# Spreading a decay by transfers from DRAM instead of products with ones, and moving a pair's loads behind a weights piece

## The chip, the cores and the metric

The kernel runs on one core of one Trainium2 chip. The metric is device time in microseconds. Before the change three runs gave 350.66, 350.76 and 352.0 us; their median is 350.76 us.

## The reference, cut to what matters

Two blocks, one behind the other: a Mamba-2 scan (SSD) in chunks, and a feed-forward block with a quick GELU.

```python
batch, n_heads, seq, head_dim, d_state = (4, 8, 768, 32, 16); chunk = 32
for c in range(nc):
    la = log(clip(a))[:, :, sl];  cum = cumsum(la)          # decay a: (batch, head, seq)
    L  = exp(cum[i] - cum[j]) * causal                      # decay between two steps of a chunk
    y  = (C @ B^T * L) @ x + (C @ state) * exp(cum)         # inside the chunk + from the state
    state = exp(sum(la)) * state + sum_j B_j x_j exp(cum[-1] - cum[j])
x = y.transpose(0, 2, 1, 3).reshape(batch * seq, 256)       # 3072 rows
h = x @ w_in;  out = (h * sigmoid(1.702 * h)) @ w_out       # 256 -> 2048 -> 256
```

All data are float32 in meaning. The two weights come as 64-bit floats, and the kernel makes float32 of them itself.

## The kernel before

**Tiles.** The 3072 rows are worked in six groups of 512 (`TG`), and the sequence of a batch in chunks of 128 rows that hold two halves of 64. A *pair* is two such chunks, 256 rows, so a group has two pairs (`PG`) and there are twelve pairs, p0 to p11. A batch is three pairs: p0, p1 and p2 belong to batch 0. "Third pair" is p2 (in the code `PG`), "fourth pair" is p3 (`PG + 1`). Each group's scan gives `yT`, which is multiplied with `w_in` (`hidden` for group 0, a Strassen-like scheme `first` for the others), passed through Silu and multiplied with `w_out` (`project_all` for group 0, `product` for the others).

**The order is written out by hand.** Instructions stand on each engine in the order in which the program calls them, and `in_order` at the end fixes it. Lists such as `in_hidden[0]` and `in_project[0]` say which extra work stands behind the f-th step of group 0's `hidden` loop (16 steps, f = 0 to 15), or ahead of the f-th step of `project_all`. All loads of this part go through one queue, SyncE's (SP).

**Weights.** `fetch(i)` loads piece i (two transfers), `fields(i)`, `rounded(i)` and `join(i)` turn it into float32 on VectorE, with two steps on ScalarE between them (`clamp(i)`). `narrow(i)` is rounded(i), fields(i+1), join(i). Pieces 0 to 5 are `w_in`, pieces 6 to 9 are `w_out`; each of pieces 6 to 9 is 1 MB and holds four f-steps of `project_all`. Pieces, and the spread `a` of most pairs, share four buffers (tag `bits`).

**What the pair's scan needs.** `L`, the decay between two steps, for all heads in all 128 partitions (512 numbers for each half). For most pairs it is made so: `store_a` clips all of `a` (in `az`), sets the first of every 64 to zero and writes it to DRAM (`scratch`); `spread(p)` reads a pair's part back with two transfers, each spreading the same rows over 64 partitions (`a<-scratch`, 256 KB each); `decay(p)` runs one scan over it (L402) and `ends(p)` (L461) makes `Be`, B times the decay to the end of the half. For p2 it is made without DRAM: `pick_a` (L366, ScalarE) puts each head's rows beside zeros, `fan` (L412, TensorE) multiplies them with ones, which spreads them over the partitions in PSUM, and `decay_heads` (L450) scans them from there, a fourth at a time.

**Rows of a.** `since[b]` is the decay since the start of each half, by batch, in a layout of 8 heads x 16 states over the partitions. For batches 1 to 3 `spread_rows(b)` loads a's rows so spread (`af<-in_a_dram`, 384 KB), `clip_rows` clips them (L480) and moves the first of each half aside on POOL (L485, L486), `decay_rows` scans them (L493). For batch 0 the first four chunks come from `since_first`, and the last two chunks (those of p2) from `fan_since`: two products with a matrix of ones by head (L501, L530), then a copy and a scan on VectorE (`since_fanned`, L541, L543).

**What comes behind.** `turn(p)` transposes a pair's b and c on TensorE (L597, four products into one bank of PSUM, `tp`), copies them to SBUF on ScalarE (L590) and makes `CsT` from `tp` and `since` on VectorE (L667). `score` (L682) and `gain` (L713) are the products of a pair of pairs; `finish` (L821, L833) gives y; `keep_both` and `add_up` carry the states; `weigh` (L693) multiplies L with the scores.

**The queue around the change.** SP's order is: az (4 transfers, L272), piece 6, p2's b, b, c, c, x, x, scratch (2), piece 7, piece 8, p3's b, b, c, c, x, x, piece 9, p3's a (2), batch 1's af, p4's a. An issue can wait for a semaphore of an engine (a buffer that is still read) and for the landing of the eighth transfer before it. `load(p)` issues b, c and x, in two transfers each; these move rows of 64 bytes (b, c) or 128 bytes (x).

Of the kernel before, what the change touches and what calls it, by code (L numbers as in the profile page):

```python
# [16 lines left out]
P = 128  # L17
# [18 lines left out]
def kernel(  # L36
# [68 lines left out]

    az = ffn.tile([P, 4 * TG // 2], FP32, tag="mg", name="az", bufs=3)[:, :NC * P].rearrange(
        "p (c s) -> p c s", c=NC)
# [137 lines left out]
    def spread(p, held=False):  # L245

        if p - 2 in ra:
            ra[p] = ra[p - 2]
        else:
            ra[p] = words(f"a{p}").bitcast(FP32)[:, :2 * NH * H].rearrange(  # L250
                "p (k e) -> p k e", k=2)
        if held:
            nc.vector.memset(ra[p][:, 0, :1], 0.0)
        b, c = divmod(2 * p, NC)
        for i, side in enumerate(SIDES):
            nc.sync.dma_start(
                out=ra[p][side],
                in_=scratch[c:c + 2, i, b * NH:(b + 1) * NH].rearrange("c h i -> c (h i)").unsqueeze(
                    0).to_broadcast([H, 2, NH * H]))
# [3 lines left out]
    def spread_rows(b):  # L263
        raf[b] = raw.tile([P, NC, P], FP32, tag="af", name=f"af{b}", bufs=1)
        nc.sync.dma_start(out=raf[b].rearrange("p c s -> p (c s)"),
                          in_=a[b].unsqueeze(1).to_broadcast([NH, N, S]))

    def rows_a(t, queues):

        e = t.shape[1] * P  # L270
        for r in range(R):
            queues[r % len(queues)].dma_start(  # L272
                out=t[32 * r:32 * r + 32].rearrange("p c s -> p (c s)"),
                in_=a.rearrange("b h s -> (b h) s")[:, :e])

# [72 lines left out]

    starts, fans, flat = {}, {}, {}

    def clip(t, name):

        nc.vector.tensor_scalar(out=t, in0=t, scalar1=1e-6, scalar2=1.0,
                                op0=ALU.max, op1=ALU.min)
        starts[name] = const.tile([P, t.shape[1], 2], FP32, name=f"starts{name}")
        first = t.rearrange(by_chunk, s=2)[:, :, :, 0]
        nc.vector.tensor_copy(starts[name], first)
        nc.vector.memset(first, 0.0)

    def pick_a(p):  # L360

        b, c = divmod(2 * p, NC)
        X = ffn.tile([P, 2, DM], FP32, tag="ob", name=f"X{p}")
        X = fans[p] = X.rearrange("p k (q i) -> p k q i", q=Q)
        for q in range(Q):
            nc.scalar.activation(X[:, :, q], az[:, c:c + 2], AF.Copy, scale=pick[:, b, q:q + 1])  # L366


# [7 lines left out]
        fill=0.0, base=N - 1, channel_multiplier=-1)  # L376
    pick = picker("pick", NB, 1, NH)
    whose = const.tile([32 * PG, 1 + PG, NH, N], FP32, name="whose")
    nc.gpsimd.memset(whose, 1.0)
    for i, n, head in ((0, 1, PG), (1, 2, PG), (0, 0, 1)):  # L380
        t = whose[32 * i:32 * i + 32, n:n + 1]
        nc.gpsimd.affine_select(out=t, in_=t, pattern=[[-1, 1], [-head, NH], [0, N]],
                                compare_op=ALU.is_equal, fill=0.0, base=-max(n - 1, 0),
                                channel_multiplier=1)
# [22 lines left out]

    def fan(p, r, ab):

        rows = slice(32 * r, 32 * r + 32)  # L410
        for i, side in enumerate(SIDES):
            nc.tensor.matmul(out=ab[side].rearrange("p (k q i) -> p k q i", k=2, q=Q),  # L412
                             lhsT=ones[rows, side], rhs=fans[p][rows][:, :, :, side],
                             start=True, stop=True, tile_position=(32 * r, H * i),
                             skip_group_check=True)

    def fan_all(p):

        ab = area(f"ab{p}")[:, :, :2 * Q * H]
        for r in range(R):  # L420
            fan(p, r, ab[:, r])
        fan_since()
        for r in range(R):
            decay_heads(p, r, ab[:, r])
        for k in range(2):
            ends(p, k)

    def pads(n, t):
# [6 lines left out]
    def keep_busy(n, m):  # L435
# [8 lines left out]
    def decay_heads(p, r, ab):  # L444

        if r == 0:
            L = ssd.tile([P, R, 2 * Q * H], FP32, tag="L", name=f"L{p}", bufs=3)
            flat[p] = L
            Ls[p] = L.rearrange("p r (k q i) -> p k r q i", k=2, q=Q)
        nc.vector.tensor_tensor_scan(  # L450
            out=flat[p][:, r], data0=ab,
            data1=idents.rearrange("p h i -> p (h i)")[:, :2 * Q * H],
            initial=0.0, op0=ALU.mult, op1=ALU.add)

# [23 lines left out]
    def clip_rows(b):  # L478
        t = raf[b]
        nc.vector.tensor_scalar(out=t, in0=t, scalar1=1e-6, scalar2=1.0,  # L480
                                op0=ALU.max, op1=ALU.min)
        first = ssd.tile([P, NC, P], FP32, tag="first", name=f"first{b}", bufs=1)
        nc.gpsimd.memset(first, 0.0)
# [5 lines left out]
    def decay_rows(b):  # L489

        t, first = raf.pop(b), firsts.pop(b)
        since[b] = ssd.tile([P, NC, P], FP32, tag="since", name=f"since{b}")
        nc.vector.tensor_tensor_scan(  # L493
            out=since[b].rearrange("p c s -> p (c s)"), data0=t.rearrange("p c s -> p (c s)"),
            data1=first.rearrange("p c s -> p (c s)"),
            initial=0.0, op0=ALU.mult, op1=ALU.add)

    def fan_rows(t, c0, c1, o):

        o = o[:, :(c1 - c0) * P]  # L500
        nc.tensor.matmul(out=o, lhsT=whose[:32, 0].rearrange("p h n -> p (h n)"),  # L501
                         rhs=t[:32, c0:c1].rearrange("p c s -> p (c s)"), start=True,
                         stop=True, tile_position=(0, 0), skip_group_check=True)
        return o

    def since_first():
# [3 lines left out]
        for p in range(PG):  # L510
            at = slice(32 * p, 32 * p + 32)
            nc.tensor.matmul(out=rows[p],
                             lhsT=whose[at, 1 + p].rearrange("p h n -> p (h n)"),
                             rhs=cum[at].rearrange("p k s -> p (k s)"), start=True, stop=True,
                             tile_position=(32 * p, 0), skip_group_check=True)
# [4 lines left out]
    def drops():  # L520
# [3 lines left out]
                1).to_broadcast([P, Q * D, 2 * CG - 1]))  # L524

    def fan_since():
        o = bank("rows4")
        t = fanned["rows"] = fan_rows(az, CG, NC, o)
        f = fanned["starts"] = o[:, 2 * P:2 * P + 2 * (NC - CG)]
        nc.tensor.matmul(out=f, lhsT=whose[:32, 0].rearrange("p h n -> p (h n)"),  # L530
                         rhs=starts[1][:32, CG:].rearrange("p c s -> p (c s)"), start=True, stop=True,
                         tile_position=(0, 0), skip_group_check=True)

    fanned = {}

    def since_fanned():

        t, f = fanned["rows"], fanned["starts"]
        first = ssd.tile([P, NC, P], FP32, tag="first", name="first0", bufs=1)[:, CG:]
        nc.gpsimd.memset(first, 0.0)  # L540
        nc.vector.tensor_copy(first.rearrange(by_chunk, s=2)[:, :, :, 0],  # L541
                              f.rearrange("p (c s) -> p c s", s=2))
        nc.vector.tensor_tensor_scan(  # L543
            out=since[0][:, CG:].rearrange("p c s -> p (c s)"), data0=t,
            data1=first.rearrange("p c s -> p (c s)"), initial=0.0, op0=ALU.mult, op1=ALU.add)

# [37 lines left out]
    def area(name):  # L584
        return psa.tile([P, R, 4 * P], FP32, tag="cb", name=name)
# [603 lines left out]
    for i in range(2, 6):  # L1189
        fetch(i)  # L1190
    rows_a(az, (nc.sync,))
    weigh(1)
# [18 lines left out]
    join(1)  # L1211
    load(PG)


# [5 lines left out]
    def store_a():  # L1220
        clip(az, 1)
        for i, side in enumerate(SIDES):
            nc.sync.dma_start(out=scratch[:, i].rearrange("c r i -> r c i"), in_=az[:32, :, side])

    at(in_hidden[0], 5, store_a, lambda: fetch(7), lambda: fetch(8),
       lambda: load(PG + 1))
    at(in_hidden[0], 6, lambda: pick_a(PG))
    at(in_hidden[0], 9, lambda: fan_all(PG))
    at(in_hidden[0], 9, since_fanned)
    for i, k, c in ((2, 1, 1), (3, 2, 2), (4, 4, 4), (5, 6, 8), (6, 9, 12), (7, 12, 15)):  # L1230
        at(in_hidden[0], k, lambda i=i: narrow(i))
# [213 lines left out]
```

## Time and profile before

| what | time |
|---|---|
| median of three runs | 350.76 us |
| the profiled execution, its own time | 349.68 us |
| its span, first to last instruction | 347.8 us |
| VectorE busy | 253.5 us |
| ScalarE busy | 153.1 us |
| POOL busy | 12.9 us |
| granted TensorE clock | 1.0 |

The span is what the profiler shows from the first to the last instruction; the execution's own time has 1.88 us more around it. Times in the views count from the start of the span. A line of a timeline is: start, length, engine, source line, operation, what it writes and reads, shape, how many; in brackets how long the engine had been idle before it and what ended that. PE is TensorE's matmul, PEld its weight load, DVE VectorE, ACT ScalarE, SPq the queue of SyncE. The length of an issue on SPq is the time that the issuing took, not the transfer.

### The profile page before, as it was taken

The page shows a single profiled execution, that of the slowest core. Times are in us where ns is not written, and L with a number is a line of the kernel's source. Part 1 is how long each engine was busy: PE and PEld are TensorE (multiplying, and loading weights), DVE is VectorE, ACT ScalarE, POOL GpSimd, SP SyncE. Part 2 cuts the span into 40 slices and gives each one's busy share as a digit, 9 for nine tenths or more (in the row PEclk, how much of TensorE's full clock was granted, in tenths as well). Part 3 has the DMA queues.
Part 4 walks back from the last instruction along what each step waited for, and adds up shares of the span by engine and source line. Part 5 has one row for each costly group of instructions (what it writes and reads, how often), then busy time and mean ns, then how long its engine had stood idle before and what let it go on. Part 6 is the DMA issues. An engine that isn't in the chain of part 4 may idle for free.

```text
span 347.8 us, 8141 instructions
## 1 busy us (share of the span) xinstructions
PE 342.0 (98%) x3392; PEld 271.9 (78%) x3392; DVE 253.5 (73%) x479; ACT 153.1 (44%) x349; POOL 12.9 (4%) x41
## 2 busy tenths in 40 slices
PE   8899999999999999999999999999999999999996
PEld 6644444557788888888888888888888888899996
DVE  5899999998679998839995649787555654455463
ACT  5698573107354324744332543442444321554320
POOL 8300000000000100000000000000000000000000
PEclk9999999999999999999999999999999999999999
DMA  6699997435526100435613036300000300000301
GB/s 162 142 336 193 283 212 155 81 77 93 105 58 128 33 2 15 63 104 102 101 28 50 2 81 117 64 2 1 2 2 2 61 2 0 0 2 0 62 0 61
DMA packets 89980, 25.92 MB, mean 75 GB/s; under 512 B 73432, under 2 KB 87128, under 8 KB 89944
## 3 DMA queue, kind: packets, MB, share of 16 engines
q1 hardware_dynamic: 89112, 24.88, 33.3%
q10 hardware_dynamic: 832, 0.52, 0.5%
q8 instruction: 26, 0.43, 0.5%
q14 instruction: 10, 0.08, 0.1%
HBM read 22.15 MB, written 3.24 MB: 73 GB/s over the span
## 4 chain that ended last, share of the span: by engine, by line
PE 97%; ACT 1%; DVE 1%; issue 0%; DVEq 0%
PE acc L1050 28%; PE X L945 20%; PE Y L955 14%; PE h L889 10%; PE o L987 8%; PE acc L1057 7%; PE y L833 2%; PE y L821 2%; PE cb L682 2%; PE A L713 1%; PE busy L440 1%; PE ab L554 1%; PE ab L548 0%; DVE steps L735 0%; ACT steps L730 0%; ACT drop L522 0%
## 5 line engine op out<-in xcount | busy, mean ns | idle before, releaser
L950 ACT ACTIVATE ac<-X 128x256 f32<-128x256 f32 x76 | 29.1, 383 | 78.6 <-PE X L945 78.2
L1050 PE MATMUL acc<-mg,mw 128*128 128x256 f32 x192 | 54.5, 379 | 0.0
L922 ACT ACTIVATE gT<-gT 128x512 f32<-128x512 f32 (+1 forms) x76 | 39.3, 520 | 34.1 <-DVE gT L1077 33.4
L1077 DVE TENSOR_TENSOR gT<-Y,ac 128x512 f32<-128x512 f32 x38 | 26.2, 689 | 36.1 <-PE Y L955 30.5
L945 PE MATMUL X<-my,mi 128*128 128x256 f32 x152 | 45.2, 380 | 0.0
L1077 DVE TENSOR_TENSOR gT<-Y,b 128x256 f32<-128x256 f32 x38 | 15.8, 419 | 35.2 <-PE Y L955 35.2
L1050 PEld LDWEIGHTS acc<-mg,mw 128*128 128x128 f32 x192 | 36.5, 190 | 5.0
L1050 PE MATMUL acc<-gT,w_out 128*128 128x256 f32 x128 | 35.5, 379 | 0.0
L889 PE MATMUL h<-yT,w_in 128*128 128x512 f32 (+2 forms) x98 | 35.5, 518 | 0.0
L945 PEld LDWEIGHTS X<-my,mi 128*128 128x128 f32 x152 | 28.0, 190 | 4.1 <-ACT ac L950 0.4
L889 PEld LDWEIGHTS h<-yT,w_in 128*128 128x128 f32 x98 | 17.0, 190 | 16.5 <-issue 14.3
L987 PE MATMUL o<-gT,w_out 128*128 128x512 f32 x64 | 28.6, 597 | 0.0
L913 DVE TENSOR_TENSOR mg<-gT 128x512 f32<-128x512 f32 x40 | 27.2, 681 | 0.0
L1050 PEld LDWEIGHTS acc<-gT,w_out 128*128 128x128 f32 x128 | 24.2, 190 | 3.4 <-ACT yT L860 0.2
L950 ACT ACTIVATE b<-X 128x256 f32<-128x256 f32 x38 | 14.6, 384 | 20.0 <-PE X L945 19.6
L945 PE MATMUL X<-yT,w_in 128*128 128x256 f32 x76 | 23.2, 389 | 0.0
L945 PE MATMUL X<-my,w_in 128*128 128x256 f32 x76 | 22.7, 382 | 0.2 <-issue 0.2
L955 PE MATMUL Y<-yT,w_in 128*128 128x256 f32 x76 | 22.7, 381 | 0.0
L955 PE MATMUL Y<-my,mi 128*128 128x256 f32 x76 | 22.6, 379 | 0.0
L955 PE MATMUL Y<-yT,mi 128*128 128x256 f32 x76 | 22.5, 379 | 0.0
L987 PEld LDWEIGHTS o<-gT,w_out 128*128 128x128 f32 x64 | 11.8, 190 | 13.2 <-issue 12.7
L402 DVE TENSOR_TENSOR_SCAN L<-a,idents 128x1024 f32<-128x1024 f32 x9 | 20.5, 2277 | 0.4 <-DMA a<-scratch 0.4
(156 smaller groups left out, 544.2 us busy)
## 6 DMA issues: line engine op xcount, KB each, us to landing
a<-scratch SPq DMA_DIRECT2D x18, 256.0 KB, 5.3
bits<-in_moe_w_out_dram SPq DMA_DIRECT2D x8, 512.0 KB, 5.4
x<-in_x_dram SPq DMA_DIRECT2D x24, 128.0 KB, 3.0
out_dram<-ob SPq DMA_DIRECT2D x40, 64.0 KB, 1.9
bits<-in_moe_w_in_dram SPq DMA_DIRECT2D x8, 256.0 KB, 4.6
bits<-in_moe_w_in_dram SPq DMA_DIRECT2D x4, 512.0 KB, 9.3
b<-in_B_dram SPq DMA_DIRECT2D x20, 64.0 KB, 3.0
af<-in_a_dram SPq DMA_DIRECT2D x3, 384.0 KB
```

The source lines that it names most:

```text
L402: nc.vector.tensor_tensor_scan(out=L, data0=ra[p].rearrange("p k e -> p (k e)"), data1=idents.rearrange("p h i -> p (h i)"), initial=0.0, ...
L682: nc.tensor.matmul(out=s["cb"][side, r, k].rearrange("p (q i) -> p q i", q=Q), lhsT=BT[rows, k, side], rhs=CT[rows, k, :, side], start=Tru ...
L889: nc.tensor.matmul(out=h[:, cols], lhsT=w_in[:, f, k], rhs=yT[g][:, k, cols], start=(k == 0 and e == 0), stop=(k == NK - 1), skip_group_ch ...
L913: nc.vector.tensor_tensor(out=t[:, 0:2], in0=B[:, :, 1], in1=B[:, 0], op=ALU.subtract)
L922: nc.scalar.activation(o, i, AF.Silu, scale=GELU_SCALE)
L945: nc.tensor.matmul(out=s["X"], lhsT=lhsT, rhs=rhs, start=i == "1", stop=i == "4", skip_group_check=True)
L950: nc.scalar.activation(copy, s["X"], AF.Copy)
L955: nc.tensor.matmul(out=o, lhsT=lhsT, rhs=rhs, start=s.pop("new", False), stop=i != "5", skip_group_check=True)
L987: nc.tensor.matmul(out=o[c], lhsT=w_out[:, c, f], rhs=gT[g, f // 2][:, f % 2], start=(f == 0), stop=(f == NF - 1), skip_group_check=True)
L1050: nc.tensor.matmul(out=acc[g][0][i][:, cols], lhsT=w, rhs=h[:, cols], start=(j == 0 and k == 0 and (i, 0) in begins), stop=(j == NF // 2 - ...
L1057: nc.tensor.matmul(out=o[k] if type(o) is list else o[:, cols], lhsT=h[:, cols], rhs=w, start=(j == 0 and (i, k) in begins), stop=(j == NF ...
L1077: nc.vector.tensor_tensor(out=o, in0=v, in1=w, op=ALU.add)
```

## The change

Three things are done, all in the first 60 us.

1. The spread of p2's `a` and of batch 0's last two chunks of rows is no longer made by products. `az` shrinks from four copies in 128 partitions to one in 32, with one load instead of four. `pick_a`, `fan`, `fan_all`, `decay_heads`, `fan_rows`, `fan_since`, `since_fanned`, `clip` and the tile `pick` go. p2's `a` is read back from `scratch` with `spread(PG)` into a buffer of the tag `yT`, and scanned by `decay(PG)` ahead of `fields(9)`. Batch 0's last rows come with `spread_rows(0)` (256 columns, 128 KB), issued right behind `load(PG)`, and `clip_rows(0)`, `decay_rows(0)` stand where the products' scans stood.
2. `load(PG + 1)`, p3's b, c and x, moves from behind piece 8 to behind piece 9 in SP's queue.
3. At the first step of `project_all` the order on VectorE becomes rounded(8), join(8), fold_ident(1), decay(PG), fields(9); before it was rounded(8), fold_ident(1), fields(9), join(8).

SP's order after is: az (1), piece 6, p2's b, b, c, c, x, x, af of batch 0 (1), scratch (2), piece 7, piece 8, p2's a (2), piece 9, p3's b, b, c, c, x, x, p3's a (2), batch 1's af, p4's a.

```diff
     def spread(p, held=False):
-        if p - 2 in ra:
+        if p == PG:
+            ra[p] = ffn.tile([P, NK, TG], FP32, tag="yT", name=f"a{p}").rearrange(
+                "p (k x) s -> p k (x s)", k=2)
+        elif p - 2 in ra and p - 2 > PG:
             ra[p] = ra[p - 2]
...
     def spread_rows(b):
-        raf[b] = raw.tile([P, NC, P], FP32, tag="af", name=f"af{b}", bufs=1)
+        c = 0 if b else CG
+        raf[b] = raw.tile([P, NC, P], FP32, tag="af", name=f"af{b}", bufs=1)[:, c:]
         nc.sync.dma_start(out=raf[b].rearrange("p c s -> p (c s)"),
-                          in_=a[b].unsqueeze(1).to_broadcast([NH, N, S]))
+                          in_=a[b, :, c * P:].unsqueeze(1).to_broadcast([NH, N, S - c * P]))
...
-    rows_a(az, (nc.sync,))
+    nc.sync.dma_start(out=az.rearrange("p c s -> p (c s)"), in_=a.rearrange("b h s -> (b h) s"))
...
     load(PG)
+    spread_rows(0)
...
     def store_a():
-        clip(az, 1)
+        nc.vector.tensor_scalar(out=az, in0=az, scalar1=1e-6, scalar2=1.0, op0=ALU.max, op1=ALU.min)
+        nc.vector.memset(az.rearrange(by_chunk, s=2)[:, :, :, 0], 0.0)
         for i, side in enumerate(SIDES):
-            nc.sync.dma_start(out=scratch[:, i].rearrange("c r i -> r c i"), in_=az[:32, :, side])
-    at(in_hidden[0], 5, store_a, lambda: fetch(7), lambda: fetch(8),
-       lambda: load(PG + 1))
-    at(in_hidden[0], 6, lambda: pick_a(PG))
-    at(in_hidden[0], 9, lambda: fan_all(PG))
-    at(in_hidden[0], 9, since_fanned)
+            nc.sync.dma_start(out=scratch[:, i].rearrange("c r i -> r c i"), in_=az[:, :, side])
+    at(in_hidden[0], 5, store_a, lambda: fetch(7), lambda: fetch(8))
+    at(in_hidden[0], 6, lambda: spread(PG))
+    at(in_hidden[0], 9, lambda: clip_rows(0), lambda: decay_rows(0))
...
-    at(in_hidden[0], 9, lambda: spread(PG + 1), lambda: spread_rows(1))
+    at(in_hidden[0], 9, lambda: load(PG + 1), lambda: spread(PG + 1), lambda: spread_rows(1))
...
-    at(in_project[0], 0, lambda: turn(PG), lambda: rounded(8), lambda: fold_ident(1),
-       lambda: fields(9), lambda: join(8))
+    at(in_project[0], 0, lambda: turn(PG), lambda: rounded(8), lambda: join(8),
+       lambda: fold_ident(1), lambda: decay(PG), lambda: fields(9))
```

More of the change, by code (lines that the diff above doesn't have):

```diff
@@ L103 @@
     dram = ctx.enter_context(tc.tile_pool(name="dram", bufs=1, space=bass.MemoryType.DRAM))
-    az = ffn.tile([P, 4 * TG // 2], FP32, tag="mg", name="az", bufs=3)[:, :NC * P].rearrange(
+    az = ffn.tile([P, 4 * TG // 2], FP32, tag="mg", name="az", bufs=3)[:32, :NC * P].rearrange(
         "p (c s) -> p c s", c=NC)
@@ L263, in spread_rows @@
     def spread_rows(b):
-        raf[b] = raw.tile([P, NC, P], FP32, tag="af", name=f"af{b}", bufs=1)
+        c = 0 if b else CG
+        raf[b] = raw.tile([P, NC, P], FP32, tag="af", name=f"af{b}", bufs=1)[:, c:]
         nc.sync.dma_start(out=raf[b].rearrange("p c s -> p (c s)"),
-                          in_=a[b].unsqueeze(1).to_broadcast([NH, N, S]))
[L268 to L274, printed above, removed]
+                          in_=a[b, :, c * P:].unsqueeze(1).to_broadcast([NH, N, S - c * P]))
     for r in range(R):
@@ L347 @@
         data1=cum.rearrange("p k s -> p (k s)"), initial=0.0, op0=ALU.mult, op1=ALU.add)
[L349 to L366, printed above, removed]
+    flat = {}
     same = ssd.tile([P, NH, D], FP32, tag="BT", name="same")
@@ L376 @@
         fill=0.0, base=N - 1, channel_multiplier=-1)
-    pick = picker("pick", NB, 1, NH)
-    whose = const.tile([32 * PG, 1 + PG, NH, N], FP32, name="whose")
+    whose = const.tile([32 * PG, PG, NH, N], FP32, name="whose")
     nc.gpsimd.memset(whose, 1.0)
[L380 to L383, printed above, removed]
+    for n in range(PG):
+        t = whose[32 * n:32 * n + 32, n:n + 1]
+        nc.gpsimd.affine_select(out=t, in_=t, pattern=[[-1, 1], [-PG, NH], [0, N]],
+                                compare_op=ALU.is_equal, fill=0.0, base=-n,
                                 channel_multiplier=1)
@@ L406, in decay @@
             ends(p, k)
[L408 to L426, printed above, removed]
     def pads(n, t):
@@ L442, in keep_busy @@
                              start=True, stop=True, skip_group_check=True)
[L444 to L453, printed above, removed]
     def ends(p, k):
@@ L481, in clip_rows @@
                                 op0=ALU.max, op1=ALU.min)
-        first = ssd.tile([P, NC, P], FP32, tag="first", name=f"first{b}", bufs=1)
+        first = ssd.tile([P, NC, P], FP32, tag="first", name=f"first{b}", bufs=1)[:, NC - t.shape[1]:]
         nc.gpsimd.memset(first, 0.0)
@@ L491, in decay_rows @@
         t, first = raf.pop(b), firsts.pop(b)
-        since[b] = ssd.tile([P, NC, P], FP32, tag="since", name=f"since{b}")
+        if b not in since:
+            since[b] = ssd.tile([P, NC, P], FP32, tag="since", name=f"since{b}")
         nc.vector.tensor_tensor_scan(
-            out=since[b].rearrange("p c s -> p (c s)"), data0=t.rearrange("p c s -> p (c s)"),
+            out=since[b][:, NC - t.shape[1]:].rearrange("p c s -> p (c s)"), data0=t.rearrange("p c s -> p (c s)"),
             data1=first.rearrange("p c s -> p (c s)"),
             initial=0.0, op0=ALU.mult, op1=ALU.add)
[L498 to L504, printed above, removed]
     def since_first():
@@ L512, in since_first @@
             nc.tensor.matmul(out=rows[p],
-                             lhsT=whose[at, 1 + p].rearrange("p h n -> p (h n)"),
+                             lhsT=whose[at, p].rearrange("p h n -> p (h n)"),
                              rhs=cum[at].rearrange("p k s -> p (k s)"), start=True, stop=True,
@@ L524, in drops @@
                 1).to_broadcast([P, Q * D, 2 * CG - 1]))
[L526 to L545, printed above, removed]
     def mask(t, new):
```

## The prediction

> **What bounds the kernel now.** I read the page first (engines and chain), then the chain of waits between 33 and 66 us, where the edits lie, then VectorE's and SyncE's timelines there, and last the transfer rates of two stretches.
>
> ```profile
> PE 342.0 (98%) x3392; PEld 271.9 (78%) x3392; DVE 253.5 (73%) x479; ACT 153.1 (44%) x349; POOL 12.9 (4%) x41
> PE 97%; ACT 1%; DVE 1%; issue 0%; DVEq 0%
> ```
>
> TensorE is busy for 98% of the span and is 97% of the chain that ended last. So a TensorE instruction that goes is worth its time, unless TensorE then waits for something that it never met before.
>
> ```profile
> 35.31 0.62 PE ab L412 x16
> 35.93 0.62 PE rows L501 x2
> 36.55 0.12 PE rows L530 x2
> 36.67 10.50 PE h L889 x24
> ...
> 51.04 0.44 PE tp L597 x4
> ...
> 64.63 0.72 PE A L713 x47
> ```
>
> Chain of waits: start, length, work. The three upper rows are the products that go. After them come two places where TensorE needs somebody else: the transposes of the fourth pair (51.04, they need its b and c loads) and gain (64.63, L713).
>
> ```profile
> 37.66 2.43 DVE L450 TENSOR_TENSOR_SCAN L<-ab,idents 128x256 f32<-128x256 f32 x4
> 40.12 0.50 DVE L461 TENSOR_TENSOR Be<-b,L 128x128 f32<-128x128 f32 x2
> 41.34 1.20 DVE L208 SCALAR_TENSOR_TENSOR m<-bits,m 128x1024 f32<-128x1024 uint32 x1
> ...
> 51.28 0.42 DVE L667 TENSOR_TENSOR CsT<-tp,since 128x256 f32<-128x256 f32 x1 [0.38 <-PE tp L597]
> ...
> 57.26 2.28 DVE L402 TENSOR_TENSOR_SCAN L<-a,idents 128x1024 f32<-128x1024 f32 x1
> 59.57 0.49 DVE L461 TENSOR_TENSOR Be<-b,L 128x128 f32<-128x128 f32 x2
> 59.98 0.55 DVE L480 TENSOR_SCALAR af<-af 128x768 f32<-128x768 f32 x1
> 61.09 1.76 DVE L493 TENSOR_TENSOR_SCAN since<-af,first 128x768 f32<-128x768 f32 x1 [0.55 <-POOL af L486]
> 62.98 0.42 DVE L667 TENSOR_TENSOR CsT<-tp,since 128x256 f32<-128x256 f32 x1
> ```
>
> VectorE here runs nearly without a gap; from 37.66 to 63.40 its three idle pieces are 0.38, 0.21 (before the last weights piece, 53.65) and 0.55. It is a second chain just behind TensorE's.
>
> ```profile
> 35.42 2.11 SPq L180 DMA_DIRECT2D bits<-in_moe_w_out_dram  x4
> 37.58 3.48 SPq L150 DMA_DIRECT2D b<-in_B_dram  x2
> 41.10 3.01 SPq L150 DMA_DIRECT2D c<-in_C_dram  x2
> ...
> 45.72 1.08 SPq L180 DMA_DIRECT2D bits<-in_moe_w_out_dram  x2
> 46.90 1.30 SPq L256 DMA_DIRECT2D a<-scratch  x2
> ```
>
> ```profile
> 48.50:50.50 2.00, 2.00 (x6) 0.81 (x5) 1.97 (x2) 1.97 (x4) 0.00 (x0) 1.00 1.04 355
> 51.00:56.50 5.50, 5.50 (x18) 2.63 (x17) 4.97 (x7) 2.34 (x3) 0.00 (x0) 1.00 1.05 190
> ```
>
> The last two columns are the DMA engines' busy share and GB/s. Both stretches are full (1.04, 1.05), yet weights (48.5 to 50.5) come at 355 GB/s and the spreads of a and af (51.0 to 56.5) at 190.
>
> **The change, step by step.** Times "after" are estimates from these rows; a shift is after minus before for the same work.
>
> *Products removed.* From 35.31 to 36.67 TensorE does nothing else, and the next h needs only a bank that ScalarE has freed. Shift of TensorE from there: -1.36. ScalarE's two picks (L366, 0.91 at 33.11) go too; ScalarE then has idle gaps at 38 to 43, so they are worth nothing more. Three of the four az loads go from SP (0.46 each) and POOL's set-up of pick; SP spends that on af0 (0.7) and a's two issues (1.3). All of it lies beside TensorE.
>
> *VectorE up to the third pair's CsT (L667 at 51.28).* The copy of starts (slot 32.71 to 32.94, 0.23) goes. The work from 37.66 to 41.34 (3.68) becomes: clip of af0, 256 columns, between the 0.17 of a 12-column copy and the 0.55 of 768 columns, taken as 0.25; the wait for POOL's copy and memset as at 61.09, 0.55; the scan, 0.61 (its slot at 40.73). 1.41 in all, so work on the weights starts at 41.34 - 0.23 - 2.27 = 38.84. Its fields step then wants piece 7 at 39.95, which lands about 40.6 (second issue 35.92, about 4.7 to landing): 0.65 lost. Pieces 6 and 7 (4.72 and 4.84 by the timeline) end at 49.05. But CsT must wait for ScalarE's copies of tp (they end 51.25), and those follow the last h on TensorE: 51.25 - 1.36 = 49.89. So VectorE idles 0.8 and its shift there is -1.36 whatever it saved before. If af0 lands up to 0.8 late, that idle time covers it.
>
> *VectorE after that.* The third pair's scan and its two Be now stand behind join(8): 2.72 (slots of 57.26 and 59.57), less the 0.21 wait for the last piece, which comes earlier. Shift at the clip of af1: -1.36 + 2.72 - 0.21 = +1.15, so 61.13, and CsT of the fourth pair ends at 63.40 + 1.15 = 64.55. In the built program gain's second matmul waits for just that CsT (it takes over the bank of tp). Gain started at 64.63; TensorE cannot be earlier than about there. **So VectorE alone takes the 1.36 back: shift about 0.0 at gain.** Bounds: -0.3 (clip 0.17, no loss at piece 7: those fall into the idle anyway, so only ScalarE's end moves it) to +1.2 (a, af1 late, below). Later meetings have more room: finish at 72.42 waits for a weigh that ended 70.95, the next gain at 83.86 for Be that ended 82.6.
>
> *The queue.* SP's order after piece 8 is now: a of the third pair (2 issues, waiting for scratch to land), last weights piece (2), then the fourth pair's b, b, c, c, x, x, then its a, af1. So 512 KB of spread and 1 MB of weights come ahead of c; before, they came behind it. What is queued behind a's wait on SP is that whole list; SP waits there some 0.3 us only, since scratch (second issue 34.9, and small transfers land 1.9 to 2.7 after their issue) lands about when piece 8's issue ends (37.2 to 37.5).
> Before: piece 8 lands at 43.6 (issue 37.0 + 6.6 in the DMA view of that issue), the second c is issued at 43.5 and lands 2.7 later (the quickest of the four c loads: 2.7/3.9/5.1), 2.6 behind the piece. The small loads hold the queue, so c follows the last big load by that 2.6. After: 43.6 + a 512 KB at 190 GB/s (2.8) + weights 1 MB at 355 GB/s (2.9) + 2.6 = 51.9. TensorE wants it at 51.3 - 1.36 = 49.95. Stall 1.95, **shift +0.6.**
> The trace has no spread in that place, so bounds: low, a at 355 GB/s (1.5): c at 50.6, shift -0.7. High, a at the 4.0 us that the spread alone at 69.5 needed (71.5, when b had landed, to 75.5) and the weights at the 5.0 of the last piece in before (two landings 2.2 and 2.8 apart): c at 55.2, shift +3.9. I take the 190 row: same kind of transfer, same fullness.
> The Trainium skill ("DMA: Bandwidth & Descriptors", Bandwidth) puts HBM's limit per core at about 358 GB/s and tells of no slower rate for a spread. The weights row agrees, the spread's row (190) doesn't; by the page c would land at 50.6 and the shift would be -0.7.
> *Late behind c:* x, a and af1 of the fourth pair. Before, af held SP's next zB until 58.8, 7.8 after the weights' data ended (51.0). After, its data starts behind x at some 53.0, so af1 is due at 60.8, against 61.13 where VectorE clips it. Just in time; each us later is a us at gain.
>
> **Sum.** TensorE goes on when the later of both waits ends: c +0.6 (-0.7 to +3.9), gain 0.0 (-0.3 to +1.2). The later of two uncertain times lies above either; I add 0.2: **+0.8**. The profiled execution took 349.68 (span 347.8), the runs' median is 350.76, 1.08 above; the shift is the same for both: 350.5 for a profile, **351.6** for the runs. Its own range: 350.5 to 352.7.
>
> **Rivals.**
> *Gain kept.* c lands by 49.95 and CsT by 63.2: -1.36, 349.4. For it: 355 GB/s is reached elsewhere. Against: VectorE's sum needs 1.3 from nowhere. 8%.
> *Transfers hidden, VectorE alone decides.* 0.0, 350.8. For it: c at the low bound. 12%.
> *The queue costs more.* The spread runs as at 69.5 (4.0) and the weights behind it as slowly as the last piece in before; c at 52.8 to 55.2, and af1 late by as much. It decides from c at 53.1 (shift +1.75). Price +1.8 to +3.9, middle +2.8: 353.6. For it: 190 GB/s held for over 5 us, also while af ran. Against: the weights' data themselves came at 355. 32%.
> The Trainium skill ("TensorE: Matmul & The Clock Gate", HAM oscillation) says that TensorE idle for over some 3.4 us drops to half clock. No gap here is near it (0.70 at 16.1, clock 1.00 in all stretches above). By the page the worst of this case would pay a little more; a 2 us stall would not.
> *The change doing nothing* is excluded: the three rows at 35.31 can't appear.
>
> **How the numbers follow.** Forecast 48%, rivals 8, 12 and 32. Half a per cent, 1.75 us, is about what a measurement of this kernel can tell from no change. Faster by more than that needs more than the 1.36 there is: 0.05 for disturbance and what I don't see. Slower by more: nearly all of the third rival and the forecast's upper edge, 0.35. Within: 0.60. The range reaches from the gain half kept (349.9) to the upper part of the third rival (354.2).
>
> **What would show it.** Right: no ab, rows4 rows at 35.3; the h row runs through; a gap of 1 to 3 us on TensorE before the second tp, ended by DMA c; VectorE idle near 49 for ScalarE; a's scan just after join(8); gain within 1 us of 64.6. Wrong: no gap at tp (the queue is faster), a gap at gain of over 1 us (af1 late or VectorE slower), or a gap at the first product with w_out (piece 6 or 7 late).

## The result, and the profile after

| | before | changed |
|---|---|---|
| median of 6 runs, us | 350.98 | 356.00 |
| all runs, us | 350.52 to 352.00 | 352.76, then 355.78 to 356.64 |
| profiled execution, us (span) | 349.68 (347.8) | 356.08 (354.1) |

The ratio is 1.0136, with a 95% interval of 1.0110 to 1.0161: slower by some 5 us, where 0.8 was forecast. In the five executions of the changed kernel that took 355.78 us and more, the granted clock of TensorE is 0.989 to 0.995 on average; in the one of 352.76 us it is 1.00.

The page of the changed kernel: busy time by engine, the granted clock in 40 slices, and the shares of the chain that ended last.

```profile
PE 344.6 (97%) x3372; PEld 272.5 (77%) x3372; DVE 253.7 (72%) x475; ACT 152.4 (43%) x347; POOL 12.1 (3%) x37
...
PEclk9999996999999999999999999999999999999999
...
PE 87%; DVE 4%; SPq 4%; DMA 3%; issue 1%; ACT 0%; POOL 0%; DVEq 0%; POOLq 0%
```

Twenty matmul records are gone (3392 to 3372), yet TensorE is busy 2.6 us longer (342.0 to 344.6), and one slice (53 to 62 us) has a clock of 0.6. The chain that ended last was 97% TensorE; now some 11% of it belong to VectorE, to SyncE's queue and to transfers. So something waits now that did not, and something runs slower. TensorE's timeline shows both: start, length, work, and in brackets the idle time before it and what ended it.

```profile
47.32 3.67 PE L905 MATMUL o<-gT,w_out 128*128 128x512 f32 x8 [0.41 <-DVE w_out L228]
53.05 0.62 PE L515 MATMUL tp<-ident,b 128*128 128x128 f32 x2 [2.06 <-DMA b<-in_B_dram]
54.60 0.48 PE L515 MATMUL tp<-ident,c 128*128 128x128 f32 x1 [0.93 <-DMA c<-in_C_dram]
55.38 0.47 PE L515 MATMUL tp<-ident,c 128*128 128x128 f32 x1 [0.31 <-DMA c<-in_C_dram]
55.66 14.80 PE L905 MATMUL o<-gT,w_out 128*128 128x512 f32 x28
70.39 1.21 PE L600 MATMUL cb<-CT,BT 32*64 32x128 f32 x64
71.53 0.79 PE L631 MATMUL A<-x,Be 64*32 64x64 f32 x56
```

From 50.99 to 55.66 TensorE does four short transposes of the fourth pair and waits for its b and c between them. Then 28 products take 14.80 us, where the same 28 took 12.18 before. Gain (the last row) starts at 71.53; before it was 64.56. The windows view of that stretch says why the products are slow: after the length come the busy times of the five engines, then the granted clock, the DMA share and GB/s.

```profile
50.69:54.10 3.41, 0.92 (x3) 0.28 (x2) 3.01 (x4) 1.59 (x4) 0.00 (x0) 1.00 0.68 71
54.10:60.93 6.83, 6.02 (x9) 2.63 (x10) 6.72 (x8) 0.57 (x1) 0.00 (x0) 0.50 0.93 151
```

In 3.41 us TensorE was busy for 0.92, and in the 6.83 us behind them its clock was half. SyncE's queue shows why the loads came so late.

```profile
36.25 2.15 SPq L180 DMA_DIRECT2D bits<-in_moe_w_out_dram  x4
38.49 2.63 SPq L259 DMA_DIRECT2D a<-scratch  x2
41.18 1.59 SPq L180 DMA_DIRECT2D bits<-in_moe_w_out_dram  x2
42.82 7.05 SPq L150 DMA_DIRECT2D b<-in_B_dram  x2
49.91 3.08 SPq L150 DMA_DIRECT2D c<-in_C_dram  x2
```

The second issue of b alone held SyncE for 5.74 us (from 44.13); it ended when a's second transfer landed (49.89). Pieces 7 and 8 landed at 43.38 and 47.78 (40.65 and 43.60 before), the last piece at 52.65, c at 55.34, x at 57.25, af1 (batch 1's rows of a) at 65.50. The last of these is VectorE's affair:

```profile
43.48 0.69 DVE L192 TENSOR_SCALAR p<-bits 128x1024 uint32<-128x1024 uint32 x1 [1.91 <-DMA bits<-in_moe_w_out_dram]
...
61.50 2.29 DVE L379 TENSOR_TENSOR_SCAN L<-a,idents 128x1024 f32<-128x1024 f32 x1 [0.58 <-DMA a<-scratch]
63.82 0.49 DVE L407 TENSOR_TENSOR Be<-b,L 128x128 f32<-128x128 f32 x2
65.53 0.56 DVE L426 TENSOR_SCALAR af<-af 128x768 f32<-128x768 f32 x1 [1.21 <-DMA af<-in_a_dram]
66.63 1.76 DVE L440 TENSOR_TENSOR_SCAN since<-af,first 128x768 f32<-128x768 f32 x1 [0.54 <-POOL af L432]
68.52 0.43 DVE L585 TENSOR_TENSOR CsT<-tp,since 128x256 f32<-128x256 f32 x1
```

CsT of the fourth pair, which gain needs, ends at 68.95 instead of 63.40. So had TensorE kept its clock it would have reached gain just when CsT was ready (68.95): 55.66, 12.1 for the products and 1.1 for cb make 68.9. Two delays of the same size lie one behind the other, and only the larger is paid: without the first one, TensorE would have waited at the second.

A ledger of this execution follows from matching the same TensorE instructions in both traces (shift, after minus before): +0.77 at 28.3, ahead of anything the change touches; -0.59 behind the removed products; +4.18 at the last of the four transposes; +6.96 behind the half clock; +6.28 at the end. Step by step, counted from its own start, that is -1.36, +4.77, +2.78 and -0.68 (small steps between 84 and 260 us): **+5.5 us**.

### The profile page after: what moved, and what is told of

Same layout as the page of the kernel before. It is cut to its first block, busy times and chain, and to the rows that moved or that the text cites. A ratio compares the mean times of both kernels' runs of the same rounds, so it can differ in the third digit from the quotient of the medians.

```text
span 354.1 us, 8091 instructions
## 1 busy us (share of the span) xinstructions
PE 344.6 (97%) x3372; PEld 272.5 (77%) x3372; DVE 253.7 (72%) x475; ACT 152.4 (43%) x347; POOL 12.1 (3%) x37
## 4 chain that ended last, share of the span: by engine, by line
PE 87%; DVE 4%; SPq 4%; DMA 3%; issue 1%; ACT 0%; POOL 0%; DVEq 0%; POOLq 0%
PE acc L968 27%; PE X L863 19%; PE Y L873 14%; PE o L905 8%; PE acc L975 7%; SPq L150 3%; DMA bits<-in_moe_w_in_dram 2%; PE y L751 2%; PE h L807 2%; PE cb L600 2%; PE y L739 1%; SPq L180 1%; PE A L631 1%; DVE w_in L228 1%; DVE p L222 1%; PE busy L397 1%
## 5 line engine op out<-in xcount | busy, mean ns | idle before, releaser
L905 PE MATMUL o<-gT,w_out 128*128 128x512 f32 x64 | 31.3, 643 | 0.4 <-DVE w_out L228 0.4
L905 PEld LDWEIGHTS o<-gT,w_out 128*128 128x128 f32 x64 | 12.9, 208 | 15.5 <-issue 14.6
L379 DVE TENSOR_TENSOR_SCAN L<-a,idents 128x1024 f32<-128x1024 f32 x10 | 22.8, 2279 | 0.8 <-DMA a<-scratch 0.8
```

The lines of the kernel that those rows point to most:

```text
L379: nc.vector.tensor_tensor_scan(out=L, data0=ra[p].rearrange("p k e -> p (k e)"), data1=idents.rearrange("p h i -> p (h i)"), initial=0.0, ...
L905: nc.tensor.matmul(out=o[c], lhsT=w_out[:, c, f], rhs=gT[g, f // 2][:, f % 2], start=(f == 0), stop=(f == NF - 1), skip_group_check=True)
```

## The experiments

Four theories had to be told apart: the loads' place in the queue ("order"), the bytes of the added transfers ("bytes"), VectorE's new order, and the clock. In the table, "wait" is TensorE's idle time at the second transposes and at gain, and "own" is the shift of the last product less the shift at 28.3, from one profile each. Three things stand beside the columns: waits for w_out (0.41 in the changed kernel, 1.91 with a2 added, 1.05 with the old order, 0.35 with rows and late loads); a half clock of 3.41 us at 18.1 with the loads back, ahead of 28.3; and gaps near 150 us, told under "Code". Runs of before, beside them, had medians of 350.73 (first four), 351.2 to 351.6 (the others).

| run | us | ratio (95%) | c, af1 land | wait | half clock | own |
|---|---|---|---|---|---|---|
| changed | 356.00 | 1.0136 (1.0110-1.0161) | 55.34, 65.50 | 3.3, 0 | 6.83 | +5.5 |
| loads back | 355.97 | 1.0151 (1.0108-1.0193) | 48.45, 63.78 | 0, 2.7 | 3.41 | +2.4 |
| no af0 | 353.75 | 1.0104 (1.0057-1.0150) | 53.23, 63.66 | 2.3, 0 | 3.41 | +2.4 |
| stall filled | 354.68 | 1.0101 (1.0065-1.0137) | 54.24, 64.02 | filled, 0 | 0 | +1.0 |
| turn later | 355.66 | 1.0153 (1.0117-1.0188) | 54.12, 64.92 | 0, 3.9 | 3.41 | +4.6 |
| no a2 | 353.14 | 1.0063 (1.0043-1.0084) | 52.13, 62.52 | 0.5, 0.2 | 0 | +0.2 |
| neither | 353.53 | 1.0053 (1.0025-1.0081) | 51.35, 61.31 | 0.9, 0 | 0 | +1.0 |
| before, loads late | 351.99 | 1.0012 (0.9991-1.0033) | 52.41, 62.81 | 0, 0 | 0 | +0.5 |
| before, a2 added | 355.85 | 1.0149 (1.0115-1.0184) | 48.51, 65.18 | 0, 1.2 | 3.41 | +5.4 |
| rows only | 351.24 | 0.9994 (0.9974-1.0014) | 49.34, 61.25 | 0, 0.8 | 0 | +0.2 |
| neither, loads back | 352.41 | 1.0015 (0.9989-1.0041) | 48.68, 61.29 | 0, 1.3 | 0 | +1.6 |
| the same, old order | 352.95 | 1.0035 (1.0015-1.0056) | 47.46, 59.77 | 0, 0 | 0 | +0.9 |
| neither, back, padded | 351.59 | 1.0021 (1.0004-1.0037) | 47.19, 59.73 | 0, 0.9 | 0 | -0.3 |
| before, shortened | 350.31 | 0.9980 (0.9962-0.9999) | 47.36, 60.06 | 0, 0 | 0 | +0.1 |
| rows, loads late | 352.82 | 1.0041 (1.0021-1.0061) | 52.64, 63.57 | 0.3, 0.7 | 0 | +2.7 |

**Loads back.** The loads stand behind piece 8 again, a behind them.

```
-    at(in_hidden[0], 5, store_a, lambda: fetch(7), lambda: fetch(8))
+    at(in_hidden[0], 5, store_a, lambda: fetch(7), lambda: fetch(8), lambda: load(PG + 1))
...
-    at(in_hidden[0], 9, lambda: load(PG + 1), lambda: spread(PG + 1), ...)
+    at(in_hidden[0], 9, lambda: spread(PG + 1), ...)
```

> The changed kernel with one part undone: the fourth pair's b, c, x loads are issued behind weights piece 8 again, ahead of the third pair's a. Theory 'order' (c comes late because it stands behind a and the last weights piece; that stall and the half clock that follows it are the whole loss): c lands by 50.5, TensorE idles under 1 us at the second transposes, clock 1.00 to the end, 350.0 to 351.5 us. Rival 'late row of a' (af1 lands after 63 whatever the order of the loads, and gain waits for VectorE's CsT): c in time, but 2 to 4 us idle of TensorE at gain, 353 to 355 us.

c came in time, and nothing was won: 1.0151. TensorE's timeline shows where the wait went.

```profile
51.65 0.38 PE L515 MATMUL tp<-ident,c 128*128 128x128 f32 x2
51.87 12.18 PE L905 MATMUL o<-gT,w_out 128*128 128x512 f32 x28
63.98 1.21 PE L600 MATMUL cb<-CT,BT 32*64 32x128 f32 x64
65.12 0.30 PE L631 MATMUL A<-x,Be 64*32 64x64 f32 x2
68.10 0.78 PE L631 MATMUL A<-x,Be 64*32 64x64 f32 x54 [2.68 <-DVE CsT L585]
```

```profile
61.90 2.29 DVE L379 TENSOR_TENSOR_SCAN L<-a,idents 128x1024 f32<-128x1024 f32 x1 [1.33 <-DMA a<-scratch]
```

TensorE runs through the transposes and stands at gain instead: the row with the 2.68 waits for VectorE's CsT (68.03). On the way to it VectorE had waited 2.20 for piece 7 and 1.33 for the fourth pair's a (61.81), the row shown last; af1 (63.78) was there when VectorE came to it (64.64). So "order" falls as the cause of the loss: the loads' place decides where TensorE waits, not whether. The profile is its quickest run (354.58); what made the other three slower (355.18 to 357.61) is in no trace.

**No af0.** A constant in place of batch 0's last rows, no transfer.

```
+        if b == 0:
+            nc.gpsimd.memset(raf[b], 0.5)
+            return
         nc.sync.dma_start(out=raf[b].rearrange("p c s -> p (c s)"),
```

> The changed kernel without the transfer of batch 0's last rows of a (a constant is written there in its place, so that part of the output is left out); loads and spread stay as changed. Theory 'eight engines' (that transfer runs on half of the DMA engines, and these bring pieces 7 and 8 some 3 to 4 us later): piece 7 lands about 41, piece 8 about 44, c about 52, stall 1.5 to 2.5 us, no half clock, 351.5 to 353 us. Rival 'order' alone: pieces 7 and 8 at 43 and 47 as in the changed kernel, c after 54, half clock again, 355.5 to 356.5 us.

Piece 7 landed at 41.41, piece 8 at 45.93, c at 53.23: between the two expectations. 128 KB less let c come 0.9 to 2.1 earlier than in the three runs with all transfers and late loads. The stall was 2.3 us and the clock halved all the same, for 3.41 us. So af0 has a price on the queue, but is not the whole loss.

**Stall filled.** Six products of 256 columns into the bank that the transposes overwrite.

```
+            for i in range(6 if p == PG + 1 else 0):
+                nc.tensor.matmul(out=t[:, :4 * H], lhsT=ones,
+                                 rhs=ones[:, :H].unsqueeze(1).to_broadcast([P, 4, H]), ...)
```

> The changed kernel with six products more of 0.44 us each just ahead of the fourth pair's transposes, written to the bank that the transposes overwrite: they lie in the stall (50.9 to 55.4) and nothing waits for them. Theory 'clock' (the stall costs some 4 us by itself, and the half clock after it 2.6 or more on top): granted clock 1.00 throughout, c still lands about 55, 352.5 to 354 us. Rival 'VectorE pays anyway' (gain would wait for af1 and CsT until 69 to 71 even at full clock): 355.5 to 356.5 us, with idle time at gain in place of the half clock.

TensorE's timeline:

```profile
51.22 2.75 PE L515 MATMUL tp<-ones 128*128 128x256 f32 x12
53.81 0.38 PE L520 MATMUL tp<-ident,b 128*128 128x128 f32 x2
54.03 0.58 PE L520 MATMUL tp<-ident,c 128*128 128x128 f32 x2
54.45 12.18 PE L910 MATMUL o<-gT,w_out 128*128 128x512 f32 x28
```

The filling is useless work of 2.75 us, and yet the 28 products are back at 12.18 and the clock is 1.00 to the end. The profile, its quickest run, took 352.72 against 356.08, the median 354.68 against 356.00 (1.0101 and 1.0136, whose intervals overlap). In the traces the half clock is the +2.78 of the ledger; the median puts it lower. Three of its four executions had a clock of 1.00, at 352.72, 355.00 and 355.09: 2.0 to 4.4 above the 350.73 of before beside them are what the late c and af1 cost at full clock.

**Turn later.** The transposes stand five steps of products later, piece 9's work on VectorE behind them.

```
-       lambda: decay_rows(1), lambda: turn(PG + 1))
-    at(in_project[0], 5, lambda: narrow(9))
+       lambda: decay_rows(1))
+    at(in_project[0], 7, lambda: turn(PG + 1), lambda: narrow(9))
```

> The changed kernel with the fourth pair's transposes five steps of products later (10 products of 0.44 us), and the last weights piece's work on VectorE behind them: TensorE reaches them at about 55.2, when c lands. Theory 'order' (only the transposes' wait for c costs): no stall at tp, gain at 63.5 to 65, 349.5 to 351.5 us. Rival 'late row of a': the stall moves to gain, which waits for af1 (65.5) and CsT (68.9): 4 us idle there, perhaps with the half clock behind it, 354 to 356.5 us.

```profile
59.33 0.38 PE L515 MATMUL tp<-ident,c 128*128 128x128 f32 x2
59.55 3.60 PE L905 MATMUL o<-gT,w_out 128*128 128x512 f32 x8
63.08 1.21 PE L600 MATMUL cb<-CT,BT 32*64 32x128 f32 x64
64.22 0.30 PE L631 MATMUL A<-x,Be 64*32 64x64 f32 x2
68.42 1.10 PE L631 MATMUL A<-x,Be 64*32 64x64 f32 x54 [3.91 <-DVE CsT L585]
```

The rival's case to the letter: no wait for c any more (54.12, the transposes are reached at 59), TensorE is at gain at 64.2, 0.3 ahead of before, and stands there for 3.91 us, the half clock behind it. (1.2 of its own +4.6 come from a gap at 156 us, see "Code".) Of two waits in a row, taking away the first gives the time to the second.

**No a2, and neither.** A constant in place of the third pair's a; then of both.

```
+        if p == PG:
+            nc.gpsimd.memset(ra[p], 0.5)
+            return
         b, c = divmod(2 * p, NC)
```

> The changed kernel without the third pair's transfer of a (512 KB; a constant is written there in its place, so that part of the output is left out); the loads stay late, batch 0's rows still come by transfer. Theory 'bytes' (the DMA engines are full from 23 to 66 us, so every transfer added puts off all that follow, c and af1 alike, by its own time, whatever the order): c at 51 to 52.5, af1 at 61 to 62.5, gain at 64.5 to 66, 350.5 to 352 us. Rival 'VectorE' (the third pair's scan behind the join, not the transfer, makes gain late): 354.5 to 356 us.

> The changed kernel without either added transfer (constants are written for the third pair's a and batch 0's last rows, so those parts of the output are left out). What is left of the change is the products' removal, VectorE's new order and the late loads. Theory 'bytes' with the products worth their time: 349.3 to 350.3 us, gain near 63.3. Rival 'VectorE takes the 1.36 back' (the prediction's third step): gain near 64.6, waiting for CsT, 350.4 to 351.4 us.

Without a2 both waits shrink to next to nothing (0.5 at the transposes, 0.2 at gain), the clock stays at 1.00, and more than half of the loss is gone (1.0063 for 1.0136). That bears out "bytes" and speaks against "VectorE", though the time was 1.1 us above the expected range. Without either, c still landed at 51.35, 0.87 after TensorE wanted it, and the median of ten runs (353.53) was 3 us above the expectation, with a wide spread (351.29 to 355.11). So there is more than the two transfers.

**Before, loads late; before, a2 added.** One part of the change each, in the kernel before.

```
+    def extra():
+        t = ffn.tile([P, NK, TG], FP32, tag="yT", name="extra")...
+        for i, side in enumerate(SIDES):
+            nc.sync.dma_start(out=t[side], in_=scratch[c:c + 2, i, ...]...)
...
+    at(in_hidden[0], 6, lambda: pick_a(PG), extra)
```

> The kernel before with one part of the change alone: the fourth pair's b, c, x behind the last weights piece. Theory 'bytes' (nothing is added, the loads are small): piece 9 lands about 47.5, c about 50, before TensorE wants it (51); 350.2 to 351.4 us. Rival 'order' (late loads cost by themselves): c after 52.5, a stall of over 1.5 us at the second transposes, 352 to 354 us.

> The kernel before with one thing added: the third pair's a is also transferred (512 KB, behind the fourth pair's loads and ahead of the last weights piece, as in the run with the loads back), into a buffer that nobody reads. All products, waits and VectorE's order stay. Theory 'bytes': the last piece, a and af1 of the fourth pair land 2.5 to 4 us later (af1 at 61.5 to 63), gain is 2 to 4 us late, 352.5 to 355 us. Rival (the transfer is hidden, VectorE's order and the products' removal make the loss): 350.3 to 351.3 us.

The late loads alone change nothing that can be measured: c landed at 52.41, when TensorE, 2.2 us late from its start in that execution, wanted it at 53.3. The added transfer alone, with every product, wait and order of before in place and nobody reading it, costs 1.49%, as much as the whole change. Its profile, VectorE first, then TensorE:

```profile
60.61 0.69 DVE L192 TENSOR_SCALAR p<-bits 128x1024 uint32<-128x1024 uint32 x1 [5.87 <-DMA bits<-in_moe_w_out_dram]
```

```profile
64.39 2.67 PE L987 MATMUL o<-gT,w_out 128*128 128x512 f32 x4 [1.91 <-DVE w_out L228]
66.99 2.01 PE L682 MATMUL cb<-CT,BT 32*64 32x128 f32 x64
68.93 0.30 PE L713 MATMUL A<-x,Be 64*32 64x64 f32 x2
70.45 0.77 PE L713 MATMUL A<-x,Be 64*32 64x64 f32 x54 [1.23 <-DVE CsT L667]
```

The last weights piece came at 60.49 (53.52 before), VectorE idled 5.87 for it, TensorE 1.91 for VectorE's join and 1.23 at gain; cb at 2.01 instead of 1.21 is the half clock. This is the run that settles the main question: **512 KB more in this queue are enough for a loss of that size.** (Taken out of the changed kernel, they are a little over half of it.) The piece came 7.0 later, though 512 KB take 2.8 at 190 GB/s; without a2 and with the loads ahead of it, it came at 52.4 to 56.4 in six profiles, so part of the 7.0 is that spread. The mean DMA share from 58 to 66 us rose from 0.54 to 0.88. The added issues also hold SyncE, for 1.3; no run separates that from the bytes.

**Rows only.** The kernel before with af0 in place of the products for batch 0's rows (0.62 + 0.12), the rest as before.

```
+        c = 0 if b else CG
+        raf[b] = raw.tile(...)[:, c:]
...
-        fan_since()
...
-    at(in_hidden[0], 9, since_fanned)
+    at(in_hidden[0], 9, lambda: clip_rows(0), lambda: decay_rows(0))
```

> The kernel before with the smaller half of the change alone: batch 0's last rows of a by transfer (128 KB, issued behind the third pair's loads) and no products for them (0.62 + 0.12 us of TensorE); the third pair's a stays with the products, the four loads of az, the loads' place and VectorE's order stay as before. Theory 'bytes' with slack (piece 7 may come 1.8 us and af1 1.2 us later before anybody waits, and 128 KB cost about 1): 0.5 to 0.7 us won, 0.998 to 0.999 of before. Rival 'no slack left' (af1 lands after 60 and gain waits): 1.001 to 1.005.

No difference: 0.9994, though the interval still holds the 0.5 to 0.7 us that were expected. In the profile the 0.74 is won at 36 us (own shift -0.74) and lost again: piece 9 came at 56.39, VectorE idled 1.35 for it, and gain waited 0.80 for CsT. That the 128 KB brought the piece so late is likely but not shown: without them it came as late as 55.71 (neither, loads back).

**Neither, loads back; the same with VectorE's old order.** No added transfer, loads behind piece 8. In the second, decay(PG) and the identities it needs stand ahead of pieces 6 and 7 again.

```
-    at(in_hidden[0], 9, lambda: clip_rows(0), lambda: decay_rows(0))
+    at(in_hidden[0], 9, lambda: fold_ident(1), lambda: decay(PG), lambda: clip_rows(0), lambda: decay_rows(0))
```

> The changed kernel without either added transfer (constants in place of the third pair's a and batch 0's last rows, left out of the output) and with the fourth pair's loads back behind piece 8. What is left of the change: the products' removal and VectorE's order. Theory 'late loads' (the run without either transfer lost its time to c, which came 0.9 us or more after TensorE): 0.996 to 1.000 of before. Rival 'VectorE's order' (the third pair's scan behind the join makes gain late): gain waits for CsT, 1.000 to 1.006.

> As the run without either transfer and with the loads back (constants in place of the third pair's a and batch 0's last rows, left out of the output), and VectorE's third-pair scan ahead of pieces 6 and 7 again, where it stood before: all that is left of the change is the 1.36 us of products removed. Theory: gain 1.2 to 1.4 us earlier than before measured from the same start, 0.995 to 0.998 of before. Rival 'something else in the changed program costs' (what the traces show as TensorE's own issue time, 1.1 us near 152): 0.999 to 1.005.

The first is the prediction's VectorE step with nothing else in the way, and its timeline shows TensorE's two places:

```profile
63.87 0.30 PE L637 MATMUL A<-x,Be 64*32 64x64 f32 x2
65.50 0.78 PE L637 MATMUL A<-x,Be 64*32 64x64 f32 x54 [1.33 <-DVE CsT L591]
...
79.34 0.62 PE L757 MATMUL y<-L,x 64*32 64x64 f32 x36 [0.33 <-issue]
...
153.14 0.80 PE L757 MATMUL y<-L,x 64*32 64x64 f32 x57 [1.40 <-issue]
```

-1.45 after the removed products, +1.51 at gain, where CsT is waited for: **VectorE takes the products' time back**. From there two waits with no releaser ("issue") make the +1.6 of the table. With the old order gain does not wait, but the first product with w_out does (1.05, VectorE now reaches piece 6 later), and the same two gaps follow: 1.0035 where 0.995 to 0.998 was expected. The theory that the removed products alone are a gain was wrong in this form; without VectorE's time they cannot be.

**Code.** In the trace, TensorE's instructions come in blocks of 16 KB by transfers of their own. In the five profiles so far with such a gap near 150 (turn later, no a2, neither, and the two just described; it cost each 1.2 to 1.6 us), the block was asked for 0.3 to 0.7 us before the y products (L757) started; in the eight others, 3.2 to 3.9 us before. The shorter program might end its blocks elsewhere, so it was padded back to its length, and the kernel before was shortened, by small products near 5 us.

```
-            pads(9, busy)
+            pads(19, busy)
```

in the run without transfers and with the loads back, and

```
-            pads(9, busy)
+            pads(0, busy)
```

in the kernel before.

> As the run without either transfer and with the loads back (constants in place of the third pair's a and batch 0's last rows, left out of the output), with ten products more of 32x32 near 5 us, where TensorE waits: they put back as many instructions as the change took out, so that TensorE's 16 KB blocks of code end where they did before. Theory 'code' (in the shorter program the block that holds the y products near 150 is asked for 0.3 to 0.7 us before they start instead of 3 to 4, and TensorE waits 1.0 to 1.4 us for it, and 0.2 to 0.3 near 78): no such gap, 1.2 to 1.5 us less than without the filling, 0.997 to 1.000 of before. Rival (the gaps come from waits for other engines): they stay, 1.000 to 1.004.

> The kernel before with the nine small products near 5 us taken out (18 matmul records, 0.37 us in which TensorE only fills a wait); nothing else. Theory 'code': the blocks of code end elsewhere, as in the changed kernel: a gap of TensorE of about 1 us with no releaser at the y products near 150, 1.001 to 1.005 of before. Rival: no gap, 0.999 to 1.001.

The gaps went with the padding: the y products at 78 run as one (x128), and the one at 150 is gone; the own shift fell from +1.6 to -0.3. In the shortened kernel one appeared:

```profile
77.76 1.50 PE L757 MATMUL y<-L,x 64*32 64x64 f32 x128
```

```profile
79.02 0.64 PE L833 MATMUL y<-L,x 64*32 64x64 f32 x38 [0.52 <-issue]
```

(padded, then shortened). But the times do not follow: padded 1.0021, unpadded 1.0015, and the shortened kernel was 0.2% faster than before, not slower, for a reason that its trace does not show. The next run has the length of before and a gap of 1.04 at 81. So that the gaps near 78 and 150 come with a late load of code is seen in each trace; that the length decides it is not shown, and in the medians the gaps do not show.

**Rows, loads late.** Rows only, the loads behind piece 9, and the second half of the identities moved from VectorE to POOL, where it took 1.29 us at 13.2.

> A version meant to beat both: the kernel before, with batch 0's last rows by transfer (0.74 us of products gone, two small products added near 5 us so that TensorE's code keeps its length), the fourth pair's loads behind the last weights piece, and the doubling of the identities (0.68 us on VectorE near 53) moved to POOL near 22 us. Theory: TensorE has 0.74 less to do, VectorE 0.9 less before gain, piece 9 is no longer late: 0.997 to 0.9985 of before. Rival 'af1 holds gain' (af1 lands after 60.5 from the same start): 0.999 to 1.003.

The rival's case: af1 landed at 63.57 (62.4 from that execution's own start), and VectorE, without the 0.68 of the identities, had to wait for it:

```profile
63.60 0.56 DVE L480 TENSOR_SCALAR af<-af 128x768 f32<-128x768 f32 x1 [1.49 <-DMA af<-in_a_dram]
```

No version beat the kernel before by more than the 0.2% of the shortened one, whose interval ends at 0.9999.

## Why the prediction was wrong

*Products removed: right.* -1.36 forecast; -1.36 in the changed kernel's trace.

*VectorE up to the third pair's CsT: the landing was mis-sized.* Piece 7 was expected at 40.6 and 0.65 lost; it came at 43.38 and 1.91 were lost. TensorE met it: 0.41 at the first product with w_out. The prediction had copied the landing from before, though it had itself put af0 ahead of the piece. The five runs of the changed kernel without af0 have piece 7 at 40.8 to 41.9, the four others with it (loads back, stall filled, turn later, no a2) at 41.6 to 43.0.

*VectorE after that: right.* "VectorE alone takes the 1.36 back: shift about 0.0 at gain". With both transfers and the late loads out of the way it was +0.06 (-1.45 and +1.51), in the padded run -0.36.

*The queue: the step that failed.* "After: 43.6 + a 512 KB at 190 GB/s (2.8) + weights 1 MB at 355 GB/s (2.9) + 2.6 = 51.9." c landed at 55.34, 53.2 to 54.2 in the three other runs with a2 ahead of it. Term by term: the last, 2.6, was 2.7. a2 costs c some 1.9 to 3.2 us (53.23 and 51.35 without af0, 54.12 to 55.34 and 52.13 with it), which holds the 2.8. The weights and a together took 4.9 in place of 5.7. Wrong is the first term, 43.6: piece 8 landed at 47.78. Three parts make these 4.2 us. The first is af0's own time on the queue, which the prediction put at nothing; it counted only SyncE's issue (0.7). In the five profiles of the changed kernel's variants without af0 piece 8 came at 44.3 to 46.0, in the five with it at 46.1 to 47.8: 1.5 later in the mean (45.2 and 46.8). The second, 1.6 (45.2 against 43.60), is the one execution of before that was taken for the rule: it is the quickest on record (349.68), its 43.60 is the earliest of all sixteen profiles, and three kernels with the queue of before up to there (shortened, a2 added, loads late) had piece 8 at 44.5 to 46.8. The last, 1.0, is this execution of the changed kernel, the latest of the five. What makes the executions differ is not shown. Before, c stood 5 us ahead of its use, so that this spread cost nothing; behind the last piece it lay on the path. (TensorE's need was read 0.2 late as well: the first transpose of c starts at 51.09, not 51.3.)

*af1: same error.* "Due at 60.8 against 61.13", from x at 53.0 and 7.8 more. The 7.8 was 8.25, but x came at 57.25. It put CsT at 68.95, so gain could not have started earlier even at full clock: the second delay was as large as the first.

*Sum.* "The later of both waits" was the right form. From its own start, c made +3.4 where +0.6 was forecast, and gain at full clock would have made +3.6 where 0.0 was. What no term held is the half clock on top, +2.78 in the profile.

*The rivals.* "The queue costs more" named the place and, with c at 52.8 to 55.2 (its terms give 53.1 to 55.2), nearly the landing; its price, +1.8 to +3.9, is what the stall costs at full clock. The only run of the changed kernel with a clock of 1.00 took 352.76, +1.8, and the filled ones +2.0 to +4.4.

The Trainium skill ("TensorE: Matmul & The Clock Gate", HAM oscillation) says that TensorE must not idle for over some 3.4 us, and the prediction concluded that a stall of 2 us was safe. The same page (What's actually happening) tells of a free-running window of 3413 ns, and the traces agree with that: every half-clock stretch but those at the start and the end of an execution is 3.41 or 6.83 us long. But a window need not be empty. The windows with TensorE busy for 1.50 of 3.41 us (a2 added), 1.18 (loads back, no af0), and 0.92 (changed) were each followed by half clock:

```profile
62.14:65.55 3.41, 1.50 (x4) 0.68 (x4) 3.38 (x3) 2.50 (x5) 0.00 (x0) 1.00 0.72 140
65.55:68.96 3.41, 3.41 (x67) 1.64 (x66) 2.83 (x5) 0.00 (x0) 0.32 (x2) 0.50 0.32 67
```

```profile
64.67:68.08 3.41, 2.58 (x59) 1.54 (x60) 3.24 (x5) 1.69 (x8) 0.74 (x1) 1.00 0.74 107
68.08:71.49 3.41, 3.41 (x10) 1.50 (x9) 3.19 (x8) 0.00 (x0) 0.00 (x0) 1.00 0.27 71
```

Above is the kernel before with a2 added: idle for 1.91 of a window, half clock in the next. Below is the run without transfers and with the loads back: busy for 2.58, no half clock. So the measurement decides: 1.9 us of idling, if they fall into one window, were enough here. 1.4 were not (busy for 2.01 of the window at 150.0, in the run with neither transfer and the loads back). One window does not fit: at 14.7 with the loads back, 1.1 us of idling were followed by half clock too, and no run shows why.

*Open:* with neither transfer the program is still 0.2 to 0.5% above before. Late loads explain part (1.0053 with, 1.0015 without, intervals that overlap), VectorE's order leaves 0.0, and the gaps beside code loads are seen but not found in the medians.

## What to carry to other kernels

Where the transfers of a stretch already fill the DMA engines, price an added one at its full time for everything behind it, and look at each waiter in turn: reordering the queue moves the wait from one to the next. A landing time read from one execution is a sample; before a load is moved behind others, set its spread over several executions against the room that is left. A stall of TensorE is to be priced with the clock that follows it: here 1.9 us of idling and more within one window were followed by a stretch of half clock that cost 1.5 to 2.8 us.

## What was not expected of the hardware

- A window of 3.41 us in which TensorE is busy for 27 to 44% was followed by half clock in each of the four cases of this stretch, and an empty one (turn later) too; windows of 59 to 86% were not, but for one of 67% (at 14.7 us, loads back), and in the changed kernel the clock stayed halved behind a window of 76% with two transposes in it.
- One SyncE issue of 64 KB in 64-byte rows (b's second) held its engine for 5.74 us while earlier transfers drained; the same issue took 2.91 before.
- The same transfers land 2 to 3 us apart in executions of kernels that do not differ ahead of them (piece 8 at 43.60, 45.81 and 46.83 in before, a2 added and loads late, issued at 37.02, 38.55 and 39.98), and the parts of one transfer land up to 3.6 us apart (piece 8 of the changed kernel: the first of its 16 semaphore steps at 44.15, the last at 47.78).
